# One seven-bank PSUM tile with kernel-declared waits, and two-bank reads, in a four-layer attention kernel

## The chip, the core and the metric

The kernel runs on one core of one Trainium2 chip. The metric is the time of one execution on the device in microseconds. Of the engines, TensorE (PE) does the matrix products and writes them to PSUM, the accumulation memory of eight banks of 512 float32 columns in each of 128 partitions; ScalarE (ACT) and VectorE (DVE) read PSUM; GpSimd (POOL) works on SBUF alone; SyncE (SP) issues the transfers. Each engine runs its own instructions in the order of the program, and semaphores make one engine wait for another.

## The reference

Four residual layers of attention, 2048 tokens, width 576, 32 heads of 18. Layers 0 and 2 have keys and values for each head (A), layers 1 and 3 share one key and one value head (B).

```python
def _A_ref(x, wqkv, wo):
    qkv = (x @ wqkv).reshape(B, S, 3, H, Dh).transpose(2, 0, 3, 1, 4)
    scores = jnp.einsum("bhqd,bhkd->bhqk", q, k) * (Dh ** -0.5)
    p = _softmax(scores, axis=-1)
    o = jnp.einsum("bhqk,bhkd->bhqd", p, v)
    return o.transpose(0, 2, 1, 3).reshape(B, S, D) @ wo
...
x = x + _A_ref(_layernorm(x, axis=-1), A_wqkv, A_wo)
x = x + _B_ref(_layernorm(x, axis=-1), B_wq, B_wk, B_wv, B_wo)
x = x + _A_ref(_layernorm(x, axis=-1), A_wqkv, A_wo)
x = x + _B_ref(_layernorm(x, axis=-1), B_wq, B_wk, B_wv, B_wo)
```

## The kernel before

A layer has three stages: projections (layer norm, transposes, queries, keys and values), attention, and the output projection, whose tail overlaps the next layer's head.

Attention is cut into windows. A window is one pair of heads (p, 16 of them) and one quarter of the queries (u, 512 of them), so a layer has 64 windows. Two things are woven together in a window. For its own pair and quarter it makes the exponentials: 16 chunks of 128 keys for each of two heads, each a matmul into one bank (`pse`, L801) that ACT reads and writes to SBUF as `pt` or `side` (L810). For the window two ahead it makes the row maxima: 32 products of 128 queries by 512 keys (`psm`, L633) that DVE reduces to one column each of `mxd` (L640), so that the exponent is bounded. Three times in a window a maximum is taken over two blocks at once: a product with a difference of keys (`psd`, L625) is put through Relu on ACT (L630), and DVE adds it to another block's product while reducing (L637). So a window has 32 exponentials and 3 Relus on ACT, and 26 plain reductions and 3 adding ones on DVE. A matmul of values by exponentials (`oacc`, L829, the eighth bank) follows some 1152 columns behind the exponentials; its sum is copied out once a window (L220). At the end of a window's maxima DVE folds them (`neg`, L779) and transposes them (L788).

The order is written out by hand (a manual schedule): `UNIT` is a window's list of steps, each with the kind for the even and the odd head (e: exponential, m: maximum, d and t: the two parts of a shared maximum), and a number after some steps says how many columns of values by exponentials follow there. The last two windows of a layer have hardly any maxima and use `ENDS` and `LAST`. `BANKS` says which bank each step takes, by age: the digit is the rank in a list of the seven banks from the longest ago taken.

What sets the waits: each bank is a tile of its own (`psum.tile([P, 512], F32, tag=f"b{b}", bufs=1)`). The framework follows each tile's accesses and puts in a wait where an access needs an earlier one: a matmul into a bank waits for the last reader of the tile that was there, and a reader waits for its matmul. Exponentials lie in SBUF tiles of one bank's size, 17 in a pool and a few in `side`.

Of the kernel before, what the change touches and what calls it, by code (L numbers as in the profile page):

```python
# [66 lines left out]
UNIT = """ee 384 em ee mm 384 em mm ee 384 me te ee 512 me me em 320 em me 192 me ed dm 448 em em me  # L67
          320 me em te 256 ee de mt 512 em mm ee 384 em mm"""

BANKS = """01 00 02 01 00 00 10 00 02 20 01 01 10 00 01 00  # L70
           00 01 01 00 01 00 00 01 01 00 01 00 02 01 00 02"""
LAST = "ee ee 640 " + "ee ee 512 " * 6 + "ee ee 384"
# [3 lines left out]
CUT_AT = 9  # L76
# [14 lines left out]
assert len(BANKS) == len(UNIT)  # L91
KINDS = [[w[a] for w, _ in UNIT if w[a] != "e"] for a in range(2)]
assert sum(n for _, n in UNIT) == 4096 and [len(k) for k in KINDS] == [16, 16]

# [17 lines left out]
def ends(first):  # L112
    left, cols = [16 - sum(w[a] == "e" for w, _ in first) for a in range(2)], 4096 - sum(n for _, n in first)
    assert left[0] == left[1] and [sum(w[a] != "e" for w, _ in first) for a in range(2)] == [CUT] * 2
    out = [list(x) for x in first]
    for i in range(left[0]):
        n = 0
        if i % 2 or i + 1 == left[0]:
            n = min(cols, 512 + (LAG - 4096 + cols) % 512)
        out.append(["ee", n])  # L120
        cols -= n
    assert not cols
    return out
# [5 lines left out]
FIRST_SHARED = 2  # L129


@with_exitstack
def tile_kernel(ctx: ExitStack, tc: tile.TileContext, A_x, A_wqkv, A_wo, B_x, B_wq, B_wk, B_wv, B_wo, out):
# [33 lines left out]
    nc.vector.memset(oacc, 0.0)  # L167
# [12 lines left out]
    sums = [cst.tile([P, 256], F32, name=f"os{i}") for i in range(2)]  # L180
    mxd = [cst.tile([P, 32], F32, name=f"mxd{i}") for i in range(2)]
# [8 lines left out]
    order = list(range(7))  # L190
# [7 lines left out]
    def oldest(rank):  # L198
        return lambda name: bank(order[rank], name)
# [11 lines left out]

    def ptile(name, shape=(P, 512), dt=F32):
        return pool.tile(list(shape), dt, tag="p", bufs=17, name=name)
# [4 lines left out]
    def copy(eng, dst, src):  # L218
        if eng is nc.scalar:
# [61 lines left out]
    def split_rows(dst, ps4, ps1):  # L281

        dst_f = dst.bitcast(F32)
        nc.scalar.activation(dst[:, 0:4], ps4, AF.Copy)
        nc.scalar.activation(dst[:, 4], ps1, AF.Copy)
        nc.vector.tensor_tensor(dst[:, 5:9], ps4, dst_f[:, 0:4], op=OP.subtract)
        nc.vector.tensor_tensor(dst[64:, 4], ps1[64:], dst_f[64:, 4], op=OP.subtract)

    def transposed(src, last, own):
        ps4, ps1 = etile("ps4"), etile("ps1") if own else oacc  # L290
        for c in range(4):
            nc.tensor.transpose(ps4[:, c * P:(c + 1) * P], src[:, c * P:(c + 1) * P], ident)
        nc.tensor.transpose(ps1[:, :P], last, ident)
        return ps4.rearrange("p (c t) -> p c t", t=P), ps1[:, :P]

    def natural(lhs, h, bank):

        ps = bank[:, :288]
        for i, (xc, wc) in enumerate(TERMS):
            nc.tensor.matmul(ps, lhs[:, xc, :], wsm[:, wc, h * 288:(h + 1) * 288],  # L300
                             start=i == 0, stop=i == len(TERMS) - 1)
# [23 lines left out]
    def stats(c):  # L325
        xc = xo[:, c, :]
        st = pool.tile([P, 2, nc.vector.BN_STATS_DIM], F32, name="st")
        for i in range(2):
            nc.vector.bn_stats(st[:, i, :], xc[:, i * 288:(i + 1) * 288])
        mv = pool.tile([P, 2], F32, bufs=4, name="mv")  # L330
        nc.vector.bn_aggr(mv, st)
# [5 lines left out]
    def scaled(c, mv, rs):  # L337
        xc = xo[:, c, :]
        xh = pool.tile([P, 640], F32, tag="xh", bufs=2, name="xh")
        nc.vector.tensor_scalar(xh[:, :D], xc, mv[:, 0:1], rs[:, 1:2], op0=OP.subtract, op1=OP.mult)  # L340
        nc.vector.tensor_scalar(xh[:, D:], xc[:, 512:], mv[:, 0:1], rs[:, 1:2], op0=OP.subtract, op1=OP.mult)
# [10 lines left out]
    def out_t(tt, hi):  # L352
# [5 lines left out]
        for i in range(2):  # L358
            copy(hi, ot[:, 2 * i:2 * i + 2], t[i])
            nc.vector.tensor_tensor(ot[:, 5 + 2 * i:7 + 2 * i], t[i], ot_f[:, 2 * i:2 * i + 2], op=OP.subtract)  # L360
        copy(hi, ot[:, 4], t[2][:, 0])
        nc.vector.tensor_tensor(ot[64:, 4], t[2][64:, 0], ot_f[64:, 4], op=OP.subtract)

    def out_w(c):
        ot = ots_[c // 2][:, :, c % 2 * P:(c % 2 + 1) * P]
        for h in range(2):
            ps = natural(ot, h, (etile if h else mtile)("psn"))
            xc = xo[:, c, h * 288:(h + 1) * 288]
            nc.vector.tensor_tensor(xc, ps, xc, op=OP.add)  # L369
# [50 lines left out]
    def out_proj(last):  # L420

        for c in range(NCH):
# [8 lines left out]
            if c % 2 == 0 and tt + 1 < 8:  # L431
                out_t(tt + 1, nc.scalar)
# [7 lines left out]
    for layer in range(4):  # L440
# [11 lines left out]
        def project(T, t, filler=False, half=None, terms=TERMS):  # L452
# [5 lines left out]
            for xc, wc in terms:  # L458
                nc.tensor.matmul(ps[:n].rearrange("p (u t) -> p u t", u=2)[:, us], w[:, wc, :n], xts[T][:, us, xc, :],  # L459
                                 start=(xc, wc) == TERMS[0], stop=(xc, wc) == (TERMS if half != 0 else TERMS_LO)[-1])  # L460
# [6 lines left out]
            nc.scalar.activation(ev[0][:n], ps[:n], AF.Copy)  # L467
# [3 lines left out]
            if filler:  # L471
                raw = ptile("evr")
                nc.scalar.activation(raw[:n], ps[:n], AF.Copy)
                nc.gpsimd.tensor_tensor(ev[1][:n], raw[:n], ev_f[0][:n], op=OP.subtract)
            else:
                nc.vector.tensor_tensor(ev[1][:n], ps[:n], ev_f[0][:n], op=OP.subtract)
            if not is_a and t == 4:
                vt = ptile("vt")
                nc.scalar.activation(vt[64:82], ps[64:82], AF.Copy)
# [9 lines left out]
        def key_diff(T, t, ps, r0, r1):  # L489

            if T == 0:
                k0s[t] = ptile("k0")
                nc.scalar.activation(k0s[t][r0:r1], ps[r0:r1], AF.Copy)
                return
            kd, lo, hi = k0s.pop(t), ptile("kl"), ptile("kh", dt=F32R)
            nc.vector.tensor_tensor(kd[r0:r1], ps[r0:r1], kd[r0:r1], op=OP.subtract)
# [10 lines left out]
        def load_kd(p):  # L507
            kds[p if is_a else 0] = kd = ptile("kd", dt=F32R)
# [18 lines left out]
        def v_trans(T, vt):  # L527
            pv = etile("psv")[:, :P]
            for u in range(4):
                nc.tensor.transpose(pv[:, u * 32:u * 32 + DH], vt[64:82, u * P:(u + 1) * P], ident[64:82, 64:82])  # L530
            nc.vector.tensor_copy(vs[0][:, 4 * T:4 * T + 4, 0, :DH],
                                  pv.rearrange("p (u e) -> p u e", u=4)[:, :, :DH])

        def project_v(c):
            return [natural(xt_of(c), h, (etile if h else mtile)("psn")).rearrange("p (e d) -> p e d", d=DH)
                    for h in range(2)]
# [4 lines left out]
        def project_v_part(c, h):  # L541
            ps = natural(xt_of(c), h, etile("psn"))
            nc.scalar.activation(v_dst(c)[:, h], ps.rearrange("p (e d) -> p e d", d=DH), AF.Copy)
# [57 lines left out]
        def max_mm(a, tile):  # L601
# [21 lines left out]
            if kind == "d":  # L623
                ps = tile("psd")
                nc.tensor.matmul(ps, q[b:b + 3 * DH, c0:c0 + P], kds[p if is_a else 0][b:b + 3 * DH],  # L625
                                 start=True, stop=True)
                r = side[:, n_r[0] % 4]
                n_r[0] += 1
                diffs[a].append(r)
                nc.scalar.activation(r, ps, AF.Relu)  # L630
            else:
                ps = tile("psm")
                nc.tensor.matmul(ps, q[b:b + KM, c0:c0 + P], k[b:b + KM, kb * 512:(kb + 1) * 512],  # L633
                                 start=True, stop=True)
                if kind == "t":
                    r = diffs[a].pop(0)
                    nc.vector.tensor_tensor_reduce(out=r, in0=ps, in1=r, scale=1.0, scalar=-3.0e38, op0=OP.add,  # L637
                                                   op1=OP.max, accum_out=mx[:, r0:r0 + 1])
                else:
                    nc.vector.reduce_max(mx[:, r0:r0 + 1], ps, axis=AX.X)  # L640
            m_count[p, u] = m_count.get((p, u), 0) + 1
            if m_count[p, u] == 32:
                max_final(p, u)

# [22 lines left out]
        if layer == 0:  # L667
            for part, tt in ((0, 1), (2, 2), (1, 3)):
                for c in range(5):
                    load_a(c, (part,), nc.scalar, nc.vector if part == 1 and c > 1 else nc.gpsimd)  # L670
# [32 lines left out]
        def last_values():  # L703

            staged = []
            for c in range(8, 12):
                pv = project_v(c)
                for h in range(2):
                    staged.append((c, h, ptile("vst", (P, 16, DH))))
                    nc.scalar.activation(staged[-1][2], pv[h], AF.Copy)  # L710
# [6 lines left out]
        def values(T):  # L717
            for c in range(4 * T, 4 * T + 4):
                for h, ps in enumerate(project_v(c)):
                    nc.scalar.activation(v_dst(c)[:, h], ps, AF.Copy)  # L720
# [56 lines left out]
        def max_final(p, u):  # L777
            neg = pool.tile([P, 8], F32, name="neg")
            nc.vector.tensor_reduce(neg, mxs.pop((p, u)).rearrange("p (b k) -> p b k", k=4), axis=AX.X, op=OP.max,  # L779
# [5 lines left out]
        def max_store(p, u):  # L785

            tr = pool.tile([P, 32], F32, name="tr")
            nc.vector.transpose(tr, nms.pop((p, u)).bitcast(F32))  # L788
# [6 lines left out]

        def exp_mm(p, u, a, kc, tile):

            q, k = ops(p)
# [182 lines left out]
```

## Time and profile before

| | |
|---|---|
| median of 3 runs | 5565.59 us (5565.21 to 5566.78) |
| the profiled execution's own time | 5566.94 us |
| its span, first to last instruction | 5565.1 us |
| granted TensorE clock | 1.000 |

The profile comes from that one execution, so sums over its rows are made against its span. Engine rows give busy time; matmul ends are modelled, and matmuls on different parts of the array run at once, so PE's busy share doesn't say how much of PE is used. In a timeline the columns are start, length, engine, source line, operation, output and inputs, count; in a group they are count, busy us, mean ns of one, and idle time ahead of them with what ended it. The views that carry the argument stand in the prediction.

### The profile page before, as it was taken

Reading aid. Unit: us, or ns where it says so; the run is one execution under the profiler, and the core shown is the slowest. Engines: PE = TensorE matmul, PEld = TensorE weight load, DVE = VectorE, ACT = ScalarE, POOL = GpSimd, SP = SyncE. Lnnn points to the kernel's source line nnn. Section 1 sums busy time; section 2 is a strip of 40 time slices with the busy share of each in tenths; the row PEclk is TensorE's granted clock in tenths of the full one; section 3 lists DMA queues with packets and bytes.
Section 4 is the critical chain, followed back from the end, with each engine's and each line's share of the span. In section 5 each row is a group of like instructions: output and inputs, shape, how many; then the busy total and the mean of one; then the engine's idle time right before and its main releaser. Section 6 shows DMA issues by size and latency. Waiting matters only on the chain. (4 is left out here: it accounts for less than half of the span.)

```text
span 5565.1 us, 157695 instructions
## 1 busy us (share of the span) xinstructions
PE 5542.7 (100%) x61788; PEld 3174.4 (57%) x61788; DVE 4992.7 (90%) x9504; ACT 4806.7 (86%) x9636; POOL 1070.9 (19%) x1731
## 2 busy tenths in 40 slices
PE   9999999999999999999999999999999999999999
PEld 8655555555855555555686555555558555555556
DVE  5799999998699999999647999999977999999995
ACT  3599999999289999999626999999992999999996
POOL 3121111112121111112221211111122211111111
PEclk9999999999999999999999999999999999999999
DMA  7321111111421110101253111111114101110102
GB/s 239 110 51 36 38 39 41 37 38 34 126 65 25 24 25 21 25 21 25 62 197 98 51 40 37 41 37 40 35 41 131 54 24 25 24 25 21 24 15 81
DMA packets 295506, 294.94 MB, mean 53 GB/s; under 512 B 151132, under 2 KB 228188, under 8 KB 285040
## 3 DMA queue, kind: packets, MB, share of 16 engines
q1 hardware_dynamic: 294760, 284.85, 18.3%
q8 instruction: 485, 7.95, 0.6%
q14 instruction: 261, 2.14, 0.1%
HBM read 158.77 MB, written 121.95 MB: 50 GB/s over the span
## 5 line engine op out<-in xcount | busy, mean ns | idle before, releaser
L640 DVE TENSOR_REDUCE mxd<-psm 128x1 f32<-128x512 f32 x6448 | 3961.0, 682 | 117.5 <-PE psm L633 95.7
L810 ACT ACTIVATE pt<-pse 128x512 f32<-128x512 f32 x6580 | 3577.0, 624 | 98.3 <-PE psm L633 33.9
L801 PE MATMUL pse<-big 64*128 64x512 f32 x8192 | 2514.4, 441 | 2.5 <-DVE mx L640 1.7
L633 PE MATMUL psm<-big 62*128 62x512 f32 x7448 | 2255.5, 434 | 1.3 <-ACT pt L810 0.5
L829 PE MATMUL oacc<-pt,vbuf 128*19 128x256 f32 (+2 forms) x24544 | 1742.6, 341 | 0.0
L801 PEld LDWEIGHTS pse<-big 64*128 64x128 f32 x8192 | 1188.7, 184 | 714.4 <-DVE mxd L640 425.5
L633 PEld LDWEIGHTS psm<-big 62*128 62x128 f32 x7448 | 1012.0, 184 | 478.7 <-DVE mxd L640 303.0
L810 ACT ACTIVATE side<-pse 128x512 f32<-128x512 f32 x1612 | 993.9, 617 | 23.5 <-PE psm L633 6.8
L829 PEld LDWEIGHTS oacc<-pt,vbuf 128*19 128x19 f32 x24544 | 628.1, 98 | 659.0 <-issue 428.6
L829 PE MATMUL oacc<-side,vbuf 128*19 128x256 f32 (+3 forms) x6016 | 774.1, 341 | 0.0
L849 POOL TENSOR_TENSOR rl<-lt,mone 128x8 f32<-128x8 f32 x256 | 420.3, 1642 | 1387.6 <-DMA lt<-os 1355.6
L829 PE MATMUL oacc<-pt,vy 128*19 128x256 f32 (+1 forms) x8192 | 564.8, 341 | 0.0
L222 POOL TENSOR_SCALAR hl<-neg 128x8 fp32r<-128x8 f32 x256 | 51.7, 202 | 2405.4 <-DVE neg L779 2405.4
L637 DVE CUSTOM_DVE_ANT_0 side<-psm,side 128x512 f32<-128x512 f32 x744 | 507.0, 681 | 0.0
L630 ACT ACTIVATE side<-psd 128x512 f32<-128x512 f32 x744 | 421.2, 608 | 0.0
L467 ACT ACTIVATE ev<-psq 128x512 fp32r<-128x512 f32 (+1 forms) x112 | 67.0, 598 | 324.6 <-PE psq L459 272.1
L829 PEld LDWEIGHTS oacc<-pt,vy 128*19 128x19 f32 x8192 | 225.4, 98 | 194.5 <-issue 134.1
L829 PEld LDWEIGHTS oacc<-side,vbuf 128*19 128x19 f32 x6016 | 238.3, 98 | 160.1 <-issue 102.9
L829 PE MATMUL oacc<-side,vy 128*19 128x256 f32 (+1 forms) x2016 | 263.0, 339 | 0.0
L625 PE MATMUL psd<-kd,big 54*128 54x512 f32 x744 | 252.8, 393 | 0.0
L300 PE MATMUL psn<-wsm,ot 128*128 128x288 f32 x1792 | 244.8, 296 | 0.4
L300 PEld LDWEIGHTS psn<-wsm,ot 128*128 128x128 f32 x1792 | 238.6, 188 | 5.5 <-issue 3.0
(90 smaller groups left out, 2836.3 us busy)
## 6 DMA issues: line engine op xcount, KB each, us to landing
big<-qk_d SPq DMA_DIRECT2D x180, 432.0 KB
qk_d<-ev SPq DMA_DIRECT2D x96, 512.0 KB
qk_d<-ev SPq DMA_DIRECT2D x120, 256.0 KB
rb<-r_d SPq DMA_DIRECT2D x1024, 18.0 KB
o_d<-os SPq DMA_DIRECT2D x1024, 18.0 KB
lt<-os SPq DMA_DIRECT2D x1024, 1.0 KB
o<-o_d SPq DMA_DIRECT2D x64, 256.0 KB
big<-m_d SPq DMA_DIRECT2D x512, 4.0 KB
```

Of the source, the lines that this page charges most:

```text
L222: eng.tensor_scalar(dst, src, 1.0, 0.0, op0=OP.mult, op1=OP.add)
L300: nc.tensor.matmul(ps, lhs[:, xc, :], wsm[:, wc, h * 288:(h + 1) * 288], start=i == 0, stop=i == len(TERMS) - 1)
L467: nc.scalar.activation(ev[0][:n], ps[:n], AF.Copy)
L625: nc.tensor.matmul(ps, q[b:b + 3 * DH, c0:c0 + P], kds[p if is_a else 0][b:b + 3 * DH], start=True, stop=True)
L630: nc.scalar.activation(r, ps, AF.Relu)
L633: nc.tensor.matmul(ps, q[b:b + KM, c0:c0 + P], k[b:b + KM, kb * 512:(kb + 1) * 512], start=True, stop=True)
L637: nc.vector.tensor_tensor_reduce(out=r, in0=ps, in1=r, scale=1.0, scalar=-3.0e38, op0=OP.add, op1=OP.max, accum_out=mx[:, r0:r0 + 1])
L640: nc.vector.reduce_max(mx[:, r0:r0 + 1], ps, axis=AX.X)
L801: nc.tensor.matmul(e, k[r:r + KE, kc * P:(kc + 1) * P], q[r:r + KE, u * 512:(u + 1) * 512], start=True, stop=True)
L810: nc.scalar.activation(pt, e, AF.Exp, scale=SCALE)
L829: nc.tensor.matmul(oacc[32 * i:32 * i + DH + 1, c0:c1], v_of(kc)[:, 2 * p + a if is_a else 0, :], pts[p, u, a, kc][:, 256 * h + c0:256 * h ...
L849: nc.gpsimd.tensor_tensor(rl, lts.pop((p, u)), mone, op=OP.pow)
```

## The change

The seven banks become one tile, `banks`, of 128 x 7 x 512. The matmuls, ACT and DVE calls go through a small wrapper, `track_banks`. It keeps, for each bank, who read it last. Every bank read by ACT or DVE is put in a group, "readers"; every matmul is declared to have no dependence on that group, except on the last readers of the bank that it writes and on those readers that made its own SBUF operands. The declaration concerns matmuls against readers. Nothing is declared between one reader and another.

With one tile, an instruction can read two neighbouring banks. A step marked with a star takes two neighbouring banks: `ee*` (six in a window, and all steps of `LAST`) has both heads' exponentials in one ACT instruction of 1024 columns, `mm*` (one in a window) both heads' maxima in one DVE instruction. Exponentials are kept in pairs, one SBUF tile of two heads (8 of them in the pool and three in `side`). The order of steps in `UNIT` is another one with the same kinds in all: 32 exponentials, 3 d and 3 t; the same 11 groups of value columns, 4096 in all. `BANKS` names the banks themselves, by four tables that take turns. `oc` has a tile of its own (`ocv`). Projections of values are read after each half, not after both.

```diff
+UNIT = """ee* mt 256 ee* em te 384 md ee* mt 512 me em em 384 me em me 384 ee* me em 448 me mm ee 320
+          md em 256 ee* dm mm 384 ee* em me 384 mm* ee em 384 me"""
+BANKS = """01 63 45 26 01 36 45 20 13 62 45 03 16 24 01 53
+           46 20 15 36 42 03 56 12 40 23 56 41 23 06 54 10
...
+LAST = "ee* ee* 640 " + "ee* ee* 512 " * 6 + "ee* ee* 384"
...
+class Engine:
...
+        def issue(*args, **kw):
+            i = f(*args, **kw)
+            self.note(i, args, kw)
+            return i
...
+def track_banks(tc, banks):
...
+    def wrote(i, args, kw):
+        for b in banks_in(args[:1]):
+            last = readers.pop(b, [])
+            own = [x for t in names(args[1:3]) for x in made.get(t, [])]
+            tc.declare_no_dep(i.ins, group="readers", keep=[x.ins for x in last + own], reason="other banks")
+            for x in last:
+                tc.add_manual_dep(i.ins, x.ins.name, mybir.DependencyInfo(mybir.DependencyClass.Sync,
+                                                                         mybir.DependencyReason.ANTI), reason="bank")
+
+    def read(i, args, kw):
+        got = banks_in([*args, *kw.values()])
+        if got:
+            tc.add_to_no_dep_group("readers", i.ins)
+            for t in names([*args[:1], *(kw[k] for k in ("out", "accum_out") if k in kw)]):
+                made.setdefault(t, []).append(i)
+            for b in got:
+                readers.setdefault(b, []).append(i)
+
+    return Engine(nc.tensor, wrote), Engine(nc.scalar, read), Engine(nc.vector, read)
...
+    banks = psum.tile([P, 7, 512], F32, name="banks")
+    pe, act, dve = track_banks(tc, banks)
...
-    def bank(b, name):
-        order.remove(b)
-        order.append(b)
-        return psum.tile([P, 512], F32, tag=f"b{b}", bufs=1, name=name)
+    def bank(b, name=None):
+        return banks[:, b]
+
+    def two_banks(b):
+        return banks[:, b:b + 2]
...
+    def two(name):
+        return pool.tile([P, 2, 512], F32, tag="p", bufs=8, name=name)
...
+                    dve.tensor_reduce(mx[:, r1:r0 + 1:r0 - r1], two_banks(b0), axis=AX.X, op=OP.max)
...
+        def exp_two(p, u, kc, b):
+
+            for a in range(2):
+                exp_row(p, u, a, kc, bank(b + a))
+            act.activation(pts_of(p, u, kc), two_banks(b), AF.Exp, scale=SCALE)
```

The rows below are the instructions as built, with the engines whose semaphore each waits for in brackets (`PE_49` is PE's, `Activation_49` ACT's, `DVE_49` DVE's; the number is of no meaning here). Because the wrapper makes the calls, all lines of the changed kernel read L153.

DVE in a window before, from the folding of the last maxima on: `mxd` is the tile of maxima, `psm` a bank, `side` the Relu's result.

```order
L779 TENSOR_REDUCE neg<-mxd_99 128x8 [waits DVE_49]
L640 TENSOR_REDUCE mxd_98<-psm 128x1 [waits PE_49] x4
L788 STREAM_TRANSPOSE tr<-hl_103 128x32 [waits DMAHW5_49,Pool_49]
L640 TENSOR_REDUCE mxd_98<-psm 128x1 [waits PE_49] x8
L637 ISA side,mxd_98<-psm,side 128x512 [waits PE_49,Activation_49]
```

The same place in the changed kernel, where `banks` is the one tile:

```order
L153 TENSOR_REDUCE neg<-mxd_100 128x8 [waits DVE_49]
L153 TENSOR_REDUCE mxd_101<-banks 128x1 [waits PE_49]
L153 TENSOR_REDUCE mxd_101<-banks 128x1 [waits PE_49,Activation_49] x2
L153 TENSOR_REDUCE mxd_101<-banks 128x1 [waits PE_49]
L153 TENSOR_REDUCE mxd_101<-banks 128x1 [waits PE_49,Activation_49]
L153 TENSOR_REDUCE mxd_101<-banks 128x1 [waits PE_49]
L153 STREAM_TRANSPOSE tr<-hl_104 128x32 [waits DMAHW0_49,Pool_49]
L153 TENSOR_REDUCE mxd_101<-banks 128x1 [waits PE_49,Activation_49] x2
L153 TENSOR_REDUCE mxd_101<-banks 128x1 [waits PE_49]
```

Before, a plain reduction waited for its matmul alone. Now reductions wait for ACT as well, at each place where ACT has read a bank since DVE's read before.

ACT in a window before, from the copy of `oacc` on (`pt` and `side` are exponentials):

```order
L220 ACTIVATE side<-oacc 128x256 [waits PE_49,Pool_49]
L810 ACTIVATE pt<-pse 128x512 [waits PE_49] x2
L810 ACTIVATE side<-pse 128x512 [waits PE_49]
L810 ACTIVATE pt<-pse 128x512 [waits PE_49,Activation_49]
L810 ACTIVATE pt<-pse 128x512 [waits PE_49] x3
```

And in the changed kernel (128x1024 is a read of two banks):

```order
L153 ACTIVATE ocv<-oacc 128x256 [waits PE_49,Pool_49]
L153 ACTIVATE side<-banks 128x512 [waits DVE_49,PE_49,Activation_49]
L153 ACTIVATE side<-banks 128x512 [waits PE_49]
L153 ACTIVATE pt<-banks 128x512 [waits DVE_49,PE_49] x2
L153 ACTIVATE pt<-banks 128x512 [waits PE_49,Activation_49]
L153 ACTIVATE pt<-banks 128x512 [waits DVE_49,PE_49]
L153 ACTIVATE side<-banks 128x1024 [waits PE_49]
```

Here too a wait for DVE has come in, wherever DVE has read a bank since ACT's read before.

More of the change, by code (lines that the diff above doesn't have):

```diff
@@ L90 @@
 BANKS = [[int(x) for x in w] for w in BANKS.split()]
-assert len(BANKS) == len(UNIT)
+BANKS = [BANKS[i:i + len(UNIT)] for i in range(0, len(BANKS), len(UNIT))]
+for row in BANKS:
+    assert all(a + 1 == b if w.endswith("*") else a != b for (w, _), (a, b) in zip(UNIT, row, strict=True))
 KINDS = [[w[a] for w, _ in UNIT if w[a] != "e"] for a in range(2)]
+PAIRS = [[0, 1], [2, 3], [4, 5]]
 assert sum(n for _, n in UNIT) == 4096 and [len(k) for k in KINDS] == [16, 16]
@@ L180, in tile_kernel @@
     sums = [cst.tile([P, 256], F32, name=f"os{i}") for i in range(2)]
+    ocv = cst.tile([P, 512], F32, name="ocv")
     mxd = [cst.tile([P, 32], F32, name=f"mxd{i}") for i in range(2)]
@@ L299, in natural @@
         for i, (xc, wc) in enumerate(TERMS):
[L300 to L301 removed]
+            pe.matmul(ps, lhs[:, xc, :], wsm[:, wc, h * 288:(h + 1) * 288],
+                   start=i == 0, stop=i == len(TERMS) - 1)
             beat(288 / 512)
```

215 lines of the change are left out of this document (130 added, 85 removed), and 5 rows, old and new, of the table BANKS.

## The prediction

> **What bounds the kernel now.** I read the page's engine line first, then the busy time by stretches, then the groups of the attention stage, then the waits, and last the timeline.
>
> ```profile
> PE 5542.7 (100%) x61788; PEld 3174.4 (57%) x61788; DVE 4992.7 (90%) x9504; ACT 4806.7 (86%) x9636; POOL 1070.9 (19%) x1731
> ...
> core 0: us, PE busy (x) PEld busy (x) DVE busy (x) ACT busy (x) POOL busy (x), PEclk, DMA share, GB/s
> 214.00:1360.00 1146.00, 1146.00 (x13841) 602.32 (x13845) 1115.04 (x2105) 1116.34 (x2230) 219.97 (x356) 1.00 0.17 42
> 1360.00:1391.00 31.00, 30.90 (x356) 14.58 (x357) 10.13 (x21) 30.69 (x65) 5.92 (x8) 1.00 0.22 62
> ```
>
> PE's 100% is a modelled overlap and says little. The two stretches are of layer 0: its 62 full windows, then its last two. In the full windows DVE is busy 1115.04 of 1146.00 us and ACT 1116.34, both 97.3 to 97.4%, **and at the same time**. A window is 1146.8/62 = 18.50 us; the foldings of maxima show it too, two windows from 700.41 to 737.40:
>
> ```profile
> 700.29 0.09 DVE L637 DVE_READ_ACCUMULATOR2_ANT mxd<- 128x1 f32 x1
> 700.41 0.19 DVE L779 TENSOR_REDUCE neg<-mxd 128x8 f32<-128x32 f32 x1
> ...
> 737.40 0.19 DVE L779 TENSOR_REDUCE neg<-mxd 128x8 f32<-128x32 f32 x1
> ```
>
> ```profile
> PEld pse L801 <- DVE mxd L640: 425.5, 1143, 0.6
> PEld psm L633 <- DVE mxd L640: 303.0, 851, 0.4
> ...
> DVE mxd L640 <- PE psm L633: 95.7, 446, 0.4
> ```
>
> PE waits for DVE to free banks (728.5 us, 2.9 us in each of 248 windows), while DVE waits for PE only 95.7 us. So DVE and ACT bound the kernel, side by side, each near full; PE has room. What is worth knowing of the change is therefore what it does to these two running at once.
>
> **The change part by part.** Durations in the attention stage and in layer 0's head:
>
> ```profile
> L640 DVE TENSOR_REDUCE mxd<-psm 128x1 f32<-128x512 f32 x1406 | 863.7, 682 | 24.9 <-PE psm L633 20.2 <-PE pse L801 3.2
> L637 DVE CUSTOM_DVE_ANT_0 side<-psm,side 128x512 f32<-128x512 f32 x162 | 110.4, 681 | 0.0
> L637 DVE DVE_READ_ACCUMULATOR2_ANT mxd<- 128x1 f32 x162 | 13.6, 84 | 0.0
> L779 DVE TENSOR_REDUCE neg<-mxd 128x8 f32<-128x32 f32 x54 | 10.1, 186 | 1.9
> ...
> L467 ACT ACTIVATE ev<-psq 128x512 fp32r<-128x512 f32 x36 | 21.5, 598 | 93.8 <-PE psq L459 78.9 <-issue 8.1 <-POOL wsm L222 4.2
> L285 ACT ACTIVATE xx<-oacc 128x128 fp32r<-128x128 f32 x8 | 2.3, 284 | 0.0
> ```
>
> and how instructions of one engine follow each other without a wait:
>
> ```profile
> 710.36 7.87 DVE L640 TENSOR_REDUCE mxd<-psm 128x1 f32<-128x512 f32 x13 [0.17 <-PE psm L633]
> ...
> 1375.85 16.48 ACT L810 ACTIVATE pt<-pse 128x512 f32<-128x512 f32 x33
> ```
>
> DVE: (7.87 - 0.68)/12 = 0.60 us from start to start, 0.08 less than one's length. ACT: (16.48 - 0.60)/32 = 0.50 us, 0.10 less than its 0.598.
>
> *The wide reads.* 512 more columns cost ACT 512 x (598 - 284)/384 = 0.42 us, so a wide exponential is 1.02 us; DVE 512 x (682 - 186)/480 = 0.53, so a wide maximum 1.21. As an estimate from these slopes, a pair saves ACT 2 x 0.50 - (0.50 + 0.42) = 0.08 us and DVE 0.07. Six and one in a window: 0.5 us of ACT, 0.07 us of DVE.
>
> *The one tile.* This is the part that decides, and the order in which the program stands shows it. PE's dependence on readers is cut down to the bank that it writes, which was so before. But between readers nothing is declared, and in the program as built each DVE read of `banks` waits for the last ACT read that stands ahead of it, whichever bank that was, and each ACT read for the last DVE read: by the waits' counts 7498 of 7498 DVE reads that follow an ACT read, and 7594 of 7613 ACT reads. Before, 253 of 7746 and 40 of 9225. So **ACT and DVE take turns** and no longer overlap. What ran side by side in 18.50 us runs one after the other.
>
> A window has 29 ACT reads (20 narrow exponentials, 6 wide, 3 Relus) and 28 DVE reads (24 plain, 1 wide, 3 adding), and 16 waits each way, so 16 turns each. Where a turn has more than one read, the follow-ons overlap: 29 - 16 = 13 on ACT, 28 - 16 = 12 on DVE. What a handing over costs stands in the projections, where DVE waits for ACT and ACT for DVE:
>
> ```profile
> 2902.25 0.60 ACT L467 ACTIVATE ev<-psq 128x512 fp32r<-128x512 f32 x1 [2.65 <-PE psq L459]
> 2902.88 0.69 DVE L476 TENSOR_TENSOR ev<-psq,ev 128x512 fp32r<-128x512 f32 x1 [2.56 <-ACT ev L467]
> ...
> 1479.04 0.69 DVE L476 TENSOR_TENSOR ev<-psq,ev 114x512 fp32r<-114x512 f32 x1
> 1479.83 0.59 ACT L479 ACTIVATE vt<-psq 18x512 f32<-18x512 f32 x1 [1.55 <-POOL kh L222]
> ```
>
> 0.03 us from ACT's end to DVE's start; 0.10 us the other way. As built, ACT's wait for DVE mostly stands in a semaphore instruction ahead of the read, and DVE's in the read itself, so I take 0.10 and 0.03, with 0.03 for both as the lower bound.
>
> One window then:
> - ACT: 23 x 0.60 + 6 x 1.02 - 13 x 0.10 = 18.6 us
> - DVE: 27 x 0.68 + 1.21 + 3 x 0.084 + 0.19 (the folding) - 12 x 0.08 = 19.0 us
> - turns: 16 x 0.03 + 16 x 0.10 = 2.1 us
> - together 39.7 us against 18.50.
>
> The copy of `oacc` and the transpose stand after the last read of a turn and lie beside the other engine's turn; without that cover they would cost 0.4 and 0.2 us a window.
>
> *PE.* Its reads become late next. A bank is written again mostly 5 to 7 reads after it was read (in a stretch of windows counted in program order 11% of the times after 4 or fewer). 5 reads are 5 x 39.7/57 = 3.5 us, and in them PE has to fit a matmul and at times a group of value columns:
>
> ```profile
> 1379.57 1.06 PE L829 MATMUL oacc<-pt,vbuf 128*19 128x256 f32 x16
> 1380.56 1.05 PE L801 MATMUL pse<-big 64*128 64x512 f32 x4
> 1381.54 1.06 PE L829 MATMUL oacc<-pt,vbuf 128*19 128x256 f32 x16
> ```
>
> A group of 512 columns takes 0.99 us with the change over, four products 0.98. That fits into 3.5 us, not always into 4 reads. Bounds: nothing, or 3 us a window (each of the 11 groups late by a quarter of a microsecond). I take 0.5, near the lower end, because most distances leave more than 1 us. So 40.2 us a window.
>
> *The rest.* The last two windows of a layer keep 7 DVE reads, now in line with ACT: about 5 us a layer, less a little for the wide reads. Ahead of the windows 56 maxima a layer run beside the projections' copies on ACT, some 8 us of them, which now come in line. Other stages wait for PE most of the time (78.9 of the 93.8 us idle ahead of `ev` above). I take 14 us a layer, 55 in all; bounds 0 and 200. The pairing of exponentials, `ocv` and values read by halves I cost at nothing: ACT's and DVE's turns cover them, and 11 pairs stand where 21 single tiles did.
>
> **Sum.** 248 full windows x (40.2 - 18.50) = 5382; 5565 + 5382 + 55 = 11,002, so **11,000 us**. The profiled execution's own time is 1.8 us over its span and 1.4 us over the median, so no correction is needed.
>
> The Trainium skill, "PSUM — Partial Sum Buffer", section Specifications (TRN2), says that ScalarE and VectorE can read PSUM in parallel at full bandwidth as long as they aren't in the same bank. The trace agrees: both 97% busy over the same 1146 us, on different banks. So by that rule the chip has no need of the new waits, and a program without them would land at the first rival below; but a semaphore in the program holds whether the chip needs it or not.
>
> **Rivals.**
>
> *Readers still overlap* (not slower). If the waits are met by the time they are reached, because the other engine's awaited read always lies long back, then DVE's load stays as the bound: 1115.04/62 = 17.98 less 0.07 = 17.9 us a window, 5565 - 248 x 0.6 = 5420 us. It decides if DVE's reads in a window start while ACT's last is still running. For it: ACT would have 0.5 us more room and PE its 2.9 us of waiting. Against it: the awaited read is the one just ahead in the program, 16 times each way. 6%.
>
> *PE joins the chain.* If banks come free too late for PE, each of the 11 groups of value columns (4096/11 = 372 columns, 0.7 us by the row above) stands in line with the readers: up to 8 us more a window, 11,000 + 248 x 7.5 = 12,860 us; half of that, 11,930. It decides once the distance to a bank's next use is under 4 reads for most groups; the count speaks against it. 8%.
>
> *PE's clock.* Every stretch that I read shows 1.00 granted, and in all of them PE is busy; none shows what happens when it waits for over half of the time. With every matmul twice as long, a group takes 2 us and a product 0.5 us more, which 3.5 us just holds; a third of the 11 groups late by 1 us gives 3.7 us a window, 11,900 us. 8%. The Trainium skill, "TensorE: Matmul & The Clock Gate", Part 1, has PE's clock halved after about 3.4 us without enough activity; the turns here would leave gaps of 1 to 2 us, so that rule is not clearly met, and no trace here shows the case.
>
> **How the numbers follow.** The forecast, strict turns with PE hidden, has 78%. Its own range: 38.6 us a window (both handings over 0.03, PE hidden), 5565 + 248 x 20.1 = 10,550; 42.7 us and 200 for the rest, 11,770. I reach up to 11,850 to take in part of the two PE cases; the first rival stays outside, as does the upper half of the other two. A change within 0.2% (11 us) can't be told from none here. Slower by more than that: 78 + 8 + 8 = 94%; faster 5%, the first rival's most; the same 1%.
>
> **What would show it.** In the changed kernel's timeline no ACT read of `banks` should overlap a DVE read; DVE and ACT should each be busy about 46 to 49% of a full window (18.6 and 19.0 of 40.2), their idle time ended by the other; two foldings of maxima should lie about 40 us apart, with 16 turns each way; a wide exponential about 1.02 us, a wide maximum 1.21. PE should wait for both readers for over half of the time. Idle time on ACT or DVE ended by PE, beyond some tenths of a microsecond a window, would mean the second rival; a granted clock under 1 the third; DVE 99% busy and windows under 18 us the first.

## The result, and the profile after

The changed kernel takes 10888.19 us (median of 4 runs, 10886.67 to 10888.88), the kernel before on the same chip 5566.18: a ratio of 1.956, 95% interval 1.9526 to 1.9594. The forecast was 11,000 us within 10,550 to 11,850. The profiled execution has a span of 10886.5 us, 1.9 us under its own time.

The page's engine line of the changed kernel, and three lines of its 40 slices (busy tenths of DVE and ACT, granted clock of PE in tenths):

```profile
PE 9161.9 (84%) x63772; PEld 4366.9 (40%) x63772; DVE 5266.2 (48%) x9260; ACT 4993.8 (46%) x8020; POOL 1072.3 (10%) x1731
...
DVE  4444444444544444444444444444445444444444
ACT  2444444445344444444424444444453444444444
PEclk9677777777877777777797767777678776776778
```

DVE did 4992.7 us of work before and does 5266.2 now, ACT 4806.7 and 4993.8. The load is nearly the same, the span twice as long: 90% and 86% have become 48% and 46%. All windows of layer 0 but the first and the last few lie in one stretch:

```profile
core 0: us, PE busy (x) PEld busy (x) DVE busy (x) ACT busy (x) POOL busy (x), PEclk, DMA share, GB/s
240.00:2690.00 2450.00, 2036.62 (x14357) 894.39 (x14361) 1182.39 (x2042) 1163.27 (x1857) 218.95 (x355) 0.71 0.08 19
```

DVE is busy for 48.3% of it and ACT for 47.5%; the two together fill 95.7%. The timeline says whether they do so at the same time. First ACT's rows from 1201 us on, then DVE's (start, length, operation, and in brackets how long the engine was idle before and what ended that):

```profile
1202.18 1.08 ACT L153 ACTIVATE side<-banks 128x512 f32<-128x512 f32 x2 [0.82 <-DVE mxd L153]
1204.68 0.60 ACT L153 ACTIVATE pt<-banks 128x512 f32<-128x512 f32 x1 [1.42 <-DVE mxd L153]
1206.69 1.09 ACT L153 ACTIVATE pt<-banks 128x512 f32<-128x512 f32 x2 [1.42 <-DVE mxd L153]
```

```profile
1203.30 1.29 DVE L153 TENSOR_REDUCE mxd<-banks 128x1 f32<-128x512 f32 x2 [1.21 <-ACT side L153]
1205.31 1.29 DVE L153 TENSOR_REDUCE mxd<-banks 128x1 f32<-128x512 f32 x2 [0.72 <-ACT pt L153]
1207.81 0.69 DVE L153 TENSOR_REDUCE mxd<-banks 128x1 f32<-128x512 f32 x1 [1.21 <-ACT pt L153]
```

They don't. ACT reads from 1202.18 to 1203.26, DVE from 1203.30 to 1204.59, ACT from 1204.68 to 1205.28, DVE from 1205.31 on, and so forth: each turn of one ends the idle time of the other. The step from ACT's end to DVE's start is 0.03 to 0.04 us here, the other way 0.09 to 0.10. Taken over the whole trace, the reads of `banks` change from ACT to DVE 4168 times and back 4167 times, and not once does the next read start before the last one of the other engine has ended; the medians of the steps are 0.032 and 0.094 us. In the stretch above there are 990 changes each way, 16 in a window, as forecast.

The waits over the whole span put sizes to it (total us, times, longest):

```profile
DVE mxd L153 <- ACT pt L153: 3022.2, 2385, 1.9
ACT pt L153 <- DVE mxd L153: 2727.4, 2025, 2.3
...
DVE mxd L153 <- ACT side L153: 1924.1, 1447, 1.9
ACT side L153 <- DVE mxd L153: 1742.9, 1486, 2.0
...
ACT pt L153 <- PE banks L153: 301.9, 194, 2.3
...
ACT side L153 <- PE banks L153: 162.3, 110, 2.0
...
ACT pt L153 <- PE oacc L153: 149.3, 105, 2.1
DVE mxd L153 <- PE banks L153: 115.6, 125, 1.7
```

Before, the windows' maxima waited for PE alone; now they wait 4946 us for ACT, and ACT's exponentials and Relus 4470 us for DVE. One sign of the prediction did not come: PE was to wait for both readers for over half of the time, and its weight loads waited 3870 us for them, 36% of the span. The foldings of maxima give the window's length. These two are 59 windows apart:

```profile
322.00 0.19 DVE L153 TENSOR_REDUCE neg<-mxd 128x8 f32<-128x32 f32 x1
...
2656.41 0.19 DVE L153 TENSOR_REDUCE neg<-mxd 128x8 f32<-128x32 f32 x1
```

(2656.41 - 322.00)/59 = 39.57 us, against 18.50 before and a forecast of 40.2.

### The profile page after: what moved, and what is told of

The parts are those of the page before. It is cut to its first block, busy times and chain, and to the rows that moved or that the text cites. A ratio compares the mean times of both kernels' runs of the same rounds, so it can differ in the third digit from the quotient of the medians.

```text
span 10886.5 us, 166054 instructions
## 1 busy us (share of the span) xinstructions
PE 9161.9 (84%) x63772; PEld 4366.9 (40%) x63772; DVE 5266.2 (48%) x9260; ACT 4993.8 (46%) x8020; POOL 1072.3 (10%) x1731
## 5 line engine op out<-in xcount | busy, mean ns | idle before, releaser
L153 PE MATMUL banks<-big 64*128 64x512 f32 (+1 forms) x15640 | 5425.1, 608 | 1639.8 <-DVE mxd L153 688.1
L153 DVE TENSOR_REDUCE mxd<-banks 128x1 f32<-128x512 f32 (+1 forms) x6200 | 4231.0, 709 | 5071.6 <-ACT pt L153 3022.2
L153 ACT ACTIVATE pt<-banks 128x512 f32<-128x512 f32 (+1 forms) x4408 | 2971.3, 704 | 3194.8 <-DVE mxd L153 2727.4
L153 PEld LDWEIGHTS banks<-big 62*128 62x128 f32 (+1 forms) x15640 | 2511.8, 250 | 4597.6 <-DVE mxd L153 1626.8
L153 ACT ACTIVATE side<-banks 128x512 f32<-128x512 f32 (+1 forms) x2916 | 1904.1, 671 | 1985.4 <-DVE mxd L153 1742.9
L153 PE MATMUL oacc<-pt,vbuf 128*19 128x256 f32 (+3 forms) x21152 | 1770.7, 442 | 0.0
L153 PE MATMUL oacc<-side,vbuf 128*19 128x128 f32 (+3 forms) x10400 | 934.9, 443 | 1.4 <-DVE ocv L153 1.4
L153 PEld LDWEIGHTS oacc<-pt,vbuf 128*19 128x19 f32 x21152 | 551.7, 116 | 825.5 <-issue 756.3
L153 PE MATMUL oacc<-pt,vy 128*19 128x128 f32 (+1 forms) x7520 | 610.1, 433 | 0.0
L153 DVE CUSTOM_DVE_ANT_0 side<-banks,side 128x512 f32<-128x512 f32 x744 | 506.6, 681 | 0.0
L153 PE MATMUL banks<-kd,big 54*128 54x512 f32 x744 | 478.2, 643 | 31.0 <-DVE mxd L153 30.8
L153 PEld LDWEIGHTS oacc<-side,vbuf 128*19 128x19 f32 x10400 | 277.0, 117 | 409.5 <-issue 374.3
L153 PEld LDWEIGHTS oacc<-pt,vy 128*19 128x19 f32 x7520 | 218.0, 120 | 312.3 <-issue 282.3
L153 PE MATMUL oacc<-side,vy 128*19 128x128 f32 (+1 forms) x3680 | 318.2, 430 | 0.0
L153 PE MATMUL banks<-wsm,ot 128*128 128x288 f32 x1792 | 243.7, 296 | 2.1 <-issue 2.1
L153 PEld LDWEIGHTS banks<-wsm,ot 128*128 128x128 f32 x1792 | 238.4, 188 | 6.4 <-issue 5.2
L153 PE MATMUL banks<-yx,big 128*128 128x512 f32 (+2 forms) x812 | 205.3, 408 | 17.3 <-ACT ev L153 11.7
L153 PE MATMUL banks<-xx,big 128*128 128x512 f32 (+1 forms) x784 | 206.7, 414 | 14.0 <-ACT evr L153 6.2
L153 PEld LDWEIGHTS banks<-kd,big 54*128 54x128 f32 x744 | 189.6, 255 | 70.6 <-DVE mxd L153 53.0
L153 DVE TENSOR_REDUCE mx<-banks 128x1 f32<-128x512 f32 x256 | 159.3, 683 | 81.7 <-PE banks L153 34.8
```

The source lines that it names most:

```text
L153: i = f(*args, **kw)
```

## The experiments

The theory on record is that the one tile makes ACT's and DVE's reads wait for each other, turn by turn, and that nothing else in the change weighs much. Its rivals: the new order of the unit, its pairs and its two-bank reads cost by themselves; PE is a link in the chain; or PE's lower clock is.

**The waits between readers taken away.** In `track_banks`, a read of ACT is declared independent of DVE's reads and the other way round, unless the two share a bank or an SBUF tile. Everything else stays as in the changed kernel.

```diff
     def read(i, args, kw):
         got = banks_in([*args, *kw.values()])
         if got:
...
+            tc.declare_no_dep(i.ins, group="dve" if mine == "act" else "act", keep=[x.ins for x in keep],
+                              reason="other banks")
+            tc.add_to_no_dep_group(mine, i.ins)
...
             tc.add_to_no_dep_group("readers", i.ins)
```

> The changed kernel with one thing more declared: an ACT read of the seven-bank tile has no dependence on DVE's reads of it and the other way round, except where both read the same bank or share an SBUF tile. Nothing else is changed; the wide reads, the pairs, the order of steps and the banks stay. If the turns between ACT and DVE are the whole loss, DVE's load of about 17.9 us a window bounds it as before and the time is about 5420 us (5380 to 5480), with ACT and DVE each over 95% busy in a full window and TensorE's clock back at 1.00. If the new order of steps, the pairs of exponentials or the wide reads cost something of their own beside the turns, it stays above 5566 us. If most of the loss came from something else (PE's clock, PE late), it stays above 8000 us.

Measured: 5567.35 us, a ratio of 1.0001 to the kernel before, interval 0.9992 to 1.001. All of the 5,321 us is gone with these waits. The stretch of full windows in layer 0, and DVE and ACT at one time in it:

```profile
240.00:1340.00 1100.00, 1100.00 (x13832) 582.56 (x13828) 1076.30 (x1968) 1053.59 (x1790) 208.71 (x339) 1.00 0.16 40
```

```profile
705.26 2.00 ACT L153 ACTIVATE pt<-banks 128x1024 f32<-128x1024 f32 x3 [0.16 <-PE banks L153]
707.14 1.10 ACT L153 ACTIVATE side<-banks 128x512 f32<-128x512 f32 x2
708.09 0.65 ACT L153 ACTIVATE pt<-banks 128x512 f32<-128x512 f32 x1
```

```profile
705.68 6.91 DVE L153 TENSOR_REDUCE mxd<-banks 128x1 f32<-128x512 f32 x11
```

Eleven maxima run without a gap while ACT reads other banks of the same tile. So the chip does let both read it at once, and the waits were the program's. But it isn't 5,420 either: the rest of the change has won nothing.

**The one tile alone.** The order, the reads and the single output tiles of the kernel before; only the seven banks are made one tile, with `track_banks` (that is, the changed kernel's declarations).

```diff
     oacc = psum.tile([P, 512], F32, name="oacc")
+    banks = psum.tile([P, 7, 512], F32, name="banks")
+    pe, act, dve = track_banks(tc, banks)
...
-        return psum.tile([P, 512], F32, tag=f"b{b}", bufs=1, name=name)
+        return banks[:, b]
```

> The kernel before with only the seven banks made one tile and the waits of matmuls declared as in the change: the old order of steps, the old banks, no wide reads, no pairs. If the one tile alone makes the turns, all of the loss is here: a window has 35 ACT reads, 29 DVE reads and 18 turns each way (36.25 in four windows' mean, counted in program order), 35 x 0.598 + 26 x 0.682 + 3 x 0.77 less the follow-ons' 17 x 0.10 and 11 x 0.08, and 18 x (0.033 + 0.094), together some 40.6 us, so 5566 + 248 x (40.6 - 18.51) + 100 = about 11,140 us (11,000 to 11,300). If the loss needs the new order or the wide reads, this stays near 5566 us.

Measured: 11144.04 us, 2.0018 (1.9978 to 2.0058); from the second folding of layer 0 to its last a window takes 40.63 us (40.6 expected). The tile alone makes the whole loss and more. The same kernel with the readers freed as above:

> The order of the kernel before, with narrow reads, its seven banks made one tile, and ACT's and DVE's reads of it declared independent where they share no bank. If the waits between readers are all that the one tile costs, this is the kernel before again: 5,566 us, within 0.2%. If one tile costs something beside them (PE's declared waits, the bookkeeping of banks), it is slower by over 11 us; the 54 us by which the new order with narrow reads and free readers stood above the kernel before (5,620) would then be found here too.

Measured: 5571.80 us, 1.0009 (0.9999 to 1.0018). The tile itself, PE's declared waits and the bookkeeping of banks can't be told from nothing.

**What the wide reads and the pairs are worth.** Two kernels in which every two-bank read is done as two, the first with the changed kernel's waits, the second with free readers:

```diff
-            act.activation(pts_of(p, u, kc), two_banks(b), AF.Exp, scale=SCALE)
+            for a in range(2):
+                act.activation(pts_of(p, u, kc)[:, a], bank(b + a), AF.Exp, scale=SCALE)
...
-                    dve.tensor_reduce(mx[:, r1:r0 + 1:r0 - r1], two_banks(b0), axis=AX.X, op=OP.max)
+                    dve.reduce_max(mx[:, r1:r1 + 1], bank(b0), axis=AX.X)
+                    dve.reduce_max(mx[:, r0:r0 + 1], bank(b0 + 1), axis=AX.X)
```

> The changed kernel with its waits as they are, but each two-bank read made as two reads of one bank. Under strict turns each instruction's time stands in line: a pair of exponentials then takes 0.50 + 0.60 against 1.02 us, a pair of maxima 0.60 + 0.68 against 1.22, so 6 x 0.08 + 0.06 = 0.5 us a window more, 248 x 0.5 = 124 us over the changed kernel's 10888, about 11,010 us. If something else than the sum of the readers set the window (PE, for example), it would not move, within 20 us.

> The same as readers_free, but each two-bank read is made as two reads of one bank, in the same places and banks. If ACT and DVE overlap, what the wide reads save is ACT's 0.5 us and DVE's 0.07 us a window. If DVE bounds a window, only DVE's 0.07 us shows: 248 x 0.07 = 17 us more than readers_free, so some 5440 us. If ACT bounds it as much, up to 248 x 0.5 = 124 us more, some 5540 us. A rival is that wide reads hold two banks for longer than a single read and so cost time: then this one is faster than readers_free.

Measured: 10998.35 us (1.9756, 1.9716 to 1.9795) and 5620.43 us (1.0094, 1.0077 to 1.0111). In turns the wide reads save 110 us, 0.44 us in each of 248 windows; the prediction's prices, 6 x 0.08 + 0.07, make 0.55. Where the engines overlap they save 53 us, 0.21 a window, and that only pays back what something else in the change costs. A last kernel of this group asks whether that is the pairs: readers free, narrow reads, and the exponentials' outputs in 22 single tiles again.

```diff
-            t = two(name)
-            halves.extend([t[:, 0], t[:, 1]])
-        t = halves.pop(0)
+        t = pool.tile([P, 512], F32, tag="p", bufs=16, name=name)
...
-                act.activation(pts_of(p, u, kc)[:, a], bank(b + a), AF.Exp, scale=SCALE)
+                act.activation(pt_of(p, u, a, kc), bank(b + a), AF.Exp, scale=SCALE)
```

> The changed order and bank table, readers free of each other, every two-bank read done as two, and the exponentials' outputs in single tiles again (16 in the pool and 6 in the side tile, as 22 of them in pairs before). If keeping the outputs in pairs is what cost the 54 us, the time goes from 5,620 back to about 5,566 us. If the new order of the unit and its banks cost it, the time stays at 5,620 us, within 11 us.

Measured: 5607.94 us, 1.0072 (1.0057 to 1.0087). Some 12 us come back, which the intervals hardly separate from none; 36 us more than the old order with one tile and free readers (5571.80) stay. So the pairs are at most a small part of the 54 us. The larger part goes with the new unit and its bank table and with the smaller edits that came along (`ocv`, values read by halves, 16 pool tiles in place of 17, three Relu buffers in place of four); no run parts these.

**One direction of the waits.** ACT's reads are freed of DVE's; DVE's still wait for ACT's.

```diff
+            if mine == "act":
+                tc.declare_no_dep(i.ins, group="dve" if mine == "act" else "act", keep=[x.ins for x in keep],
+                                  reason="other banks")
```

> The changed kernel with the waits of one direction left out: ACT's reads of the tile are declared independent of DVE's reads (but not where they share a bank or an SBUF tile), DVE's reads still wait for ACT's, some 4,300 waits instead of some 8,500. If turns need waits in both directions (ACT runs ahead in its own time, and what DVE waits for is over by then), the time is near that with both directions free, 5,570 to 5,900 us. If each wait costs its share of the loss, half of the waits leave half of it: (10,888 + 5,567)/2 = about 8,200 us.

Measured: 6843.56 us, 1.2291 (1.2267 to 1.2316). Neither: 24% of the loss is left, (6843.6 - 5567.4)/(10888.2 - 5567.4). The full windows of layer 0 (240 to 1340 us), their busy times and their waits:

```profile
240.00:1340.00 1100.00, 992.53 (x10851) 475.30 (x10849) 871.56 (x1544) 863.51 (x1404) 158.00 (x255) 1.00 0.13 33
```

```profile
PEld banks L153 <- DVE mxd L153: 286.3, 533, 1.5
...
DVE mxd L153 <- ACT pt L153: 118.5, 223, 1.0
ACT side L153 <- PE banks L153: 111.7, 189, 1.4
ACT pt L153 <- PE banks L153: 104.8, 182, 1.5
DVE mxd L153 <- ACT side L153: 102.1, 152, 1.0
```

DVE is idle for 228 us of the 1100, 221 of them ended by ACT. But ACT, which no longer waits for DVE, is idle for 236, 217 of them ended by PE, and PE waits for DVE to release banks. The theory that ACT would run ahead forgot that there are only seven banks: ACT can lead DVE no further than PE finds free banks, so the second half of the ring closes through PE. That reading is by the waits alone; no run gave it more banks.

**PE relieved.** The value products of 14 of the 16 chunks of keys are left out, with the changed kernel's waits.

```diff
-            for i in range(4) if turn[0] % 2 else range(3, -1, -1):
+            for i in [] if 0 < kc < NCH - 1 else range(4) if turn[0] % 2 else range(3, -1, -1):
```

> The changed kernel with the value products of 14 of the 16 chunks of keys left out (the output is not the attention's any more), so that TensorE has some 0.44 us x 56 x 2 fewer matmul pieces' worth of work in each window: more than half of what it does there. If PE is hidden behind the turns of ACT and DVE, at its lower clock too, the time stays at 10,888 us but for the readers' few waits for PE: 10,820 to 10,890. If PE is a link of the chain (value products between a bank's release and its next product), windows get shorter by microseconds: each microsecond is 248 us, so 10,640 us or less.

Measured: 10877.56 us, 1.9537 (1.9498 to 1.9576), 11 us or 0.1% under the changed kernel and inside its interval.

```profile
240.00:2690.00 2450.00, 1718.07 (x4947) 765.00 (x4946) 1182.69 (x2043) 1159.63 (x1856) 218.97 (x355) 0.50 0.07 18
```

Two thirds of PE's instructions are gone and its clock is down to 0.50; ACT and DVE are busy as before, to 0.3%. The 11 us are 0.04 us a window. The run lowers PE's work and its clock at once, so a gain and a loss could hide in this; but the changed kernel's own gaps, shown further below, leave no more for PE either.

**Towards a version that beats both.** With free readers the wide reads do save something, so a better order should bring it out. Four units and bank tables were tried, all with free readers: two with four wide maxima in a window, then two nearer to the first ones. (The unit of the first, told as having seven wide exponentials, has six.)

```diff
-UNIT = """ee* mt 256 ee* em te 384 md ee* mt 512 me em em 384 me em me 384 ee* me em 448 me mm ee 320
-          md em 256 ee* dm mm 384 ee* em me 384 mm* ee em 384 me"""
+UNIT = """me ee et 384 em mm* ee 512 me mm ee* 448 me dm em 384 ee* em te 384 mm* md ee* 448 md ee* mm 256 ee* me et 320 mm* ee* em 448 me mm* ee 256 me em 256"""
```

> The changed kernel with readers that share no bank free of each other, and another unit and bank table: four wide maxima in a window instead of one, seven wide exponentials instead of six, and banks given so that a pair of neighbours has long been read when its two products come. If DVE is the bound of a window once the readers are free (1076.30 of 1100 us busy there), three more wide maxima take 3 x 0.07 = 0.21 us of DVE's time out of each of 248 windows, 52 us: 5,515 us. If the order costs as much again as the first new order did (54 us against the kernel before with narrow reads), it ends at 5,567 us, the kernel before, or above.

> As more_wide_a with a third order: four wide maxima and seven wide exponentials in a window, at other places between the value products. Same forecast by the count of DVE's reads: 5,515 us. A difference between the two is what an order costs at equal load of ACT and DVE; if it is larger than 30 us, PE's waits and not DVE's load set the time.

Measured: 5861.97 us (1.0528, 1.0512 to 1.0544) and 5763.35 us (1.0352, 1.0335 to 1.0369). Both forecasts missed. In the full windows of the first (240 to 1340 us) PE waits for the copy of `oacc`:

```profile
PEld oacc L146 <- ACT ocv L146: 76.1, 56, 1.4
...
PE oacc L146 <- ACT ocv L146: 48.5, 56, 0.9
```

In those of the second DVE waits for the Relu that stands just ahead of its addition:

```profile
DVE side L146 <- ACT side L146: 37.6, 57, 0.7
```

In the first, weight load and product wait at the same time for the same copy, so the two rows are one wait, 76 us of the 1100. In the second it is 38 us. Each comes 56 or 57 times, so once in a window; the windows are 1.2 and 0.8 us longer than with the changed order. The two orders differ by 99 us; over 30 was to mean that PE's waits and not DVE's load set the time, but the second order's wait is one for ACT. The next two orders keep clear of both places:

> Readers free of each other, and a unit that keeps closer to the first ones: two wide maxima and five wide exponentials in a window, a Relu's difference read by DVE several reads after it was made, and no value products that wait for the copy of oacc straight behind it. One more wide maximum than the changed kernel is 0.07 us of DVE a window, 17 us: 5,550 us if DVE idles as much as with the changed order (24 of 1100 us). If the place of these two waits is what made the orders with four wide maxima slow, it comes out below the kernel before, 5,500 to 5,560 us; if wide maxima themselves are (two banks held for 1.2 us), above 5,600 us.

> Readers free, an order with almost every slot holding one exponential and one maximum: one wide maximum and three wide exponentials. DVE's load is that of the changed kernel, ACT's is 3 x 0.08 = 0.24 us a window more. If ACT has that room, 5,567 us as with the changed order and free readers, less what PE's even load may give: 5,500 to 5,570 us. If an order's stalls decide and not the load, it may be as far above as the two orders before.

Measured: 5613.17 us (1.0086, 1.0069 to 1.0103) and 5589.51 us (1.004, 1.0025 to 1.0055). Both lie above the ranges hoped for (5,500 to 5,560 and 5,500 to 5,570 us). Much of the loss came back, which fits the two waits as the cause of much of it. But by the mark on record, above 5,600 us, the first would speak against the wide maxima themselves; it changes the places, the number of wide maxima and the bank table at once, so the runs don't part these. It has one wide maximum more than the changed order and one wide exponential less, and is 46 us slower with free readers. DVE's load is equal or lower in all four orders; in the last two neither engine is full (1051 to 1065 us busy of 1100), so what an order leaves idle counts, by tenths of a microsecond a window. No version that beats the kernel before was found.

## Why the prediction was right, and where it wasn't

*What bounds the kernel, and that it turns into turns: right.* The step that decided was read from the program's order (each read waits for the other engine's last earlier read). The timeline shows it, and taking the waits away gives the old time back (a ratio of 1.0001).

*The price of a window: 40.2 forecast, 39.57 measured.* The prices of the reads and turns hold. The groups by shape of the changed kernel (count, busy us, mean ns), DVE's and then ACT's:

```profile
L153 DVE TENSOR_REDUCE mxd<-banks 128x1 f32<-128x512 f32 x5952 | 3926.9, 688 | 4891.7 <-ACT pt L153 2951.2 <-ACT side L153 1882.5 <-PE banks L153 48.2
...
L153 DVE TENSOR_REDUCE mxd<-banks 128x2 f32<-128x1024 f32 x248 | 304.1, 1226 | 179.9 <-ACT pt L153 71.0 <-PE banks L153 67.4 <-ACT side L153 41.6
```

```profile
L153 ACT ACTIVATE pt<-banks 128x512 f32<-128x512 f32 x3312 | 1894.0, 595 | 2463.9 <-DVE mxd L153 2227.9 <-PE oacc L153 149.3 <-PE banks L153 83.3
...
L153 ACT ACTIVATE side<-banks 128x1024 f32<-128x1024 f32 x516 | 527.4, 1022 | 354.9 <-DVE mxd L153 243.1 <-PE banks L153 111.6
```

A wide exponential is 1.02 to 1.03 us (forecast 1.02), a wide maximum 1.23 (1.21). From 240 to 2690 us, with overlapping reads of one engine counted once, ACT is busy for 18.8 us of a window and DVE for 19.1. Without the copy of `oacc` (0.38) and the transpose (0.20) that is 37.3 us; the turns are 16 x (0.032 + 0.094) = 2.0, together 39.3. The forecast had 39.7 for the same.

*The cover: taken as whole, and it wasn't.* Copy and transpose were to lie beside the other engine's turn and cost nothing. The copy lies beside work of DVE for 0.30 of its 0.38 us, the transpose beside work of ACT for only 0.02 of its 0.20. So 0.26 us stand in line, and 39.3 becomes 39.57.

*PE's lateness: a term that isn't there.* 0.5 us a window was taken, from the lengths of the value products and the distances of banks. In the stretch above one of the two engines at least is busy for 37.56 us of a window, and neither for 2.01, which is what the turns come to. Of the gaps in which neither works, what goes beyond 0.15 us makes 0.03 us a window. So hardly anything is left for PE, at its lower clock too. The relieved PE says nearly the same (0.04). The list of waits warns here: ACT's and DVE's idle times ended by PE sum to over 700 us in the rows shown above, 3 us a window, which by the sign on record would have meant the second rival; and yet taking two thirds of PE's work away changed 11 us. A wait ended by PE would mostly have lasted nearly as long for the other reader.

*The rest: too small.* 55 us was taken, within 0 to 200; it is 5321.4 - 248 x (39.57 - 18.50) = 96 us. The prediction counted a layer's last two windows, at about 5 us, and the maxima ahead of the windows, at 8. The first cost almost nothing: from a layer's last folding to its last exponential it is 26.1 to 28.8 us against 26.0, 4 us in all. The second cost twice as much as taken: from the first of these maxima to the second folding the layers lose 13.8, 21.1, 13.7 and 22.5 us, 71 in all. Some 22 us more lie elsewhere, in the projections ahead of the maxima, between the layers and at the end, and were not counted. Half of the 71 us lies between a layer's first folding and its second, here of layer 0, before and after:

```profile
194.48 0.19 DVE L779 TENSOR_REDUCE neg<-mx 128x8 f32<-128x32 f32 x1
...
218.84 0.19 DVE L779 TENSOR_REDUCE neg<-mx 128x8 f32<-128x32 f32 x1
```

```profile
206.76 0.19 DVE L153 TENSOR_REDUCE neg<-mx 128x8 f32<-128x32 f32 x1
...
242.87 0.19 DVE L153 TENSOR_REDUCE neg<-mx 128x8 f32<-128x32 f32 x1
```

24.36 us became 36.11, and the four layers together lose 38 there. The errors pull against each other: 248 x 0.63 = 156 us too much and 41 too little leave the forecast some 112 us high. That it came within about 1% is partly luck.

*The first rival's price: wrong.* "Readers still overlap" was given 5420 us, by DVE's load as the bound. With the readers free the load is what was said (1076.30 of 1100 us in windows of 18.46, so 18.1 us), but DVE is idle for the other 0.4, and the time is 5567. The step that failed is that the pairs, the order and the bank table cost nothing: the new unit with what came along takes some 36 us and the pairs perhaps 12, and the wide reads' 53 only make up for it.

*PE joins the chain; PE's clock.* The first is refuted by the relieved PE and by the gaps. Of the second, half came true: the clock fell, and in the full windows it can hardly have cost more than the 0.03 us above.

## What to carry to other kernels

When tiles are merged into one, ask first whom the framework now makes wait for whom: with its own dependencies between readers, one tile of several banks puts two engines in turn that worked side by side, and every other gain of the edit is small beside that. A declaration that frees the writer does nothing for the readers; each pair of engines on the tile needs one of its own, and with half of it 24% of the loss stayed here. Two engines that add up to about 100% of a stretch and end each other's idle time are the sign of it in a profile.

## What the runs showed of the hardware that was not expected

PE's granted clock fell as PE had less to do, without PE ever being idle for long: it is 1.00 in the full windows before and with free readers (12.1 and 12.6 matmuls per us), still 1.00 with the waits of one direction (9.9), 0.71 in those of the changed kernel (5.9) and 0.50 with the value products left out (2.0). The 0.71 is a mean: the trace's record of the clock has only stretches of 1.00 and of 0.50 there, over 300 of them from 240 to 2690 us, each a whole multiple of 3.41 us long. One product's group in the three kernels, in this order before, changed and relieved:

```profile
L801 PE MATMUL pse<-big 64*128 64x512 f32 x8192 | 2514.4, 441 | 2.5 <-DVE mx L640 1.7
```

```profile
L153 PE MATMUL banks<-big 64*128 64x512 f32 x8192 | 3529.2, 602 | 824.9 <-ACT pt L153 439.8 <-ACT side L153 222.5 <-DVE mxd L153 151.6
```

```profile
L153 PE MATMUL banks<-big 64*128 64x512 f32 x8192 | 4794.8, 739 | 1488.4 <-ACT pt L153 584.3 <-DVE mxd L153 539.3 <-ACT side L153 354.0
```

A product takes 441, 602 and 739 ns, and of the 39.57 us of a window hardly more than 0.03 can come from it. The Trainium skill, "TensorE: Matmul & The Clock Gate", Part 1, knows two states, half rate and full, and a return to half after an idle window of about 3.4 us. The two states and the length of the stretches agree. But from 240 to 2690 us no gap between the records of PE's matmuls is longer than 1.79 us in the changed kernel and 2.27 us in the relieved one, so a window that counted as idle here can't have been one without matmuls. How little PE must do in it no run here shows.
